# A second layer issued from one written list of steps, with chunk 1 transposed by DMA

## The chip, the cores and the metric

The kernel runs on one core of one Trainium2 chip. The metric is the device time of one launch in microseconds, median of three runs. Engine names are those of the profile: PE (TensorE matmul), PEld (its weight loads), DVE (VectorE), ACT (ScalarE), POOL (GpSimd), SP (SyncE, which issues every DMA of this part).

## The reference, cut to what matters

An attention-like recurrence gives 3072 rows of 384 numbers, a first gated layer (two products, their elementwise product, a third and fourth product) follows, and then the second layer, which is all that the change touches:

```python
h = x @ w_in                                  # 3072 x 384 by 384 x 1024
e = np.exp(h - np.max(h, axis=-1, keepdims=True))
solu = h * e / (np.sum(e, axis=-1, keepdims=True) + 1e-09)
ln = (solu - mean(solu)) / np.sqrt(var(solu) + 1e-06) * g_ln
out = ln @ w_out                              # 3072 x 1024 by 1024 x 384
```

## The kernel before, in words

The second layer works in 24 chunks of 128 rows. Every float32 product is made of three matmuls of split operands (high by high, high by low, low by high: lines 200 to 202, one helper). The order of each engine's instructions is the order in which the code is written; no scheduler moves them here. The work on one chunk i, with the letter that the change gives to each step, is this:

- **s**: x2 is split, high part on ACT (L842), low part on POOL (L843).
- **h**: 18 matmuls of 512 columns on PE into the accumulator `ps_h` (there are two, one for even and one for odd chunks).
- **e**: the row maximum `nm` on DVE (L855), then the exponential on ACT (L858).
- **m**: on DVE the product `p` of `ps_h` and `e` (L863; after it `ps_h` is free for chunk i+2), the statistics (L866 to L876), and two small operations on POOL.
- **c**: the mean is taken off, on ACT (L885).
- the chunk is transposed, in one of two ways. By PE, **t**: 8 transposes (L927) into `ps_p`. By DMA, **v**: ACT takes the chunk apart into 16-bit halves (L896, four copies), SP stores them in DRAM in two halves (L897, tile `pd`) and reads each half back transposed (L902, tile `e`).
- **u** (after t) or **w** (after v): the transposed chunk is split into `pt`, high part on ACT (L350, two casts), low part on DVE (L527, two subtractions).
- **o**: 24 matmuls of 384 columns on PE from `pt` into `ps_o`.
- **z**: the scaled result on ACT (L947) and its store by SP (L948).

Chunks 0 and 1 and the last one (23) were transposed by PE, chunks 2 to 22 by DMA. A loop over i issued h, e, s, m of chunk i+1, then w and o, z of an earlier chunk, then c and v of chunk i+1. Exceptions in it (`M0`, `M1`) moved w of chunks 2 and 21 and left out one o at i = 3. Before the loop, while the first layer ends, h, e, m and c of chunk 0 are issued. After the loop, and ahead of the last three results, every engine reads the flag `wok` into a register (L1214), on which a branch around a slow fallback path depends.

Of the kernel before, what the change touches and what calls it, by code (L numbers as in the profile page):

```python
# [8 lines left out]
F32 = mybir.dt.float32  # L9
# [115 lines left out]
def tile_rwkv_bilinear_solu(  # L125
# [710 lines left out]
    def pick(i):  # L836
        return pq[i % len(pq)]
# [5 lines left out]
        nc.gpsimd.tensor_sub(xl, x, f32(xh))  # L843
        return xh, xl

    def s3(x, i=0, between=None, ahead=NCH):
        xh, xl = x
        wih, wil = d2["wih"], d2["wil"]
        q = pick(i)["q"]
        ph = pick(i)["h"].tile([P, 2, NH], F32, name="ps_h", tag="ps_h")  # L850
        for hf in range(2):
            hsl = slice(hf * NH, (hf + 1) * NH)
            mm3(ph[:, hf, :], [((xh[:, kt, :], xl[:, kt, :]), (wih[:, kt, hsl], wil[:, kt, hsl])) for kt in range(KM)])
        nm = q.tile([P, 1], F32, name="nm", tag="nm")
        nc.vector.tensor_reduce(out=nm, in_=ph, axis=AX.XY, op=ALU.max, negate=True)  # L855
        e = pq[min(i % 3, 1)]["q"].tile([P, 2, NH], F32, name="e", tag=f"e{i % 3}")
        sm = q.tile([P, 1], F32, name="sm", tag="sm")
        nc.scalar.activation(e, ph, AF.Exp, bias=nm, scale=1.0, accum_out=sm)  # L858
        if between:
            between()  # L860
        split_chunk(ahead)
        p = q.tile([P, 2, NH], F32, name="p", tag="p")
        nc.vector.tensor_mul(p, ph, e)  # L863
        st = q.tile([P, 2, 6], F32, name="bst", tag="bst")
        for hf in range(2):
            nc.vector.bn_stats(st[:, hf, :], p[:, hf, :])  # L866
# [12 lines left out]
        a = q.tile([P, 1], F32, name="al", tag="al", bufs=2)
        nc.gpsimd.tensor_mul(a, rs, c1)  # L880
        return e, p, nmean, a, i

    def center(st):
        e, p, nmean, a, i = st
        nc.scalar.activation(e, p, AF.Identity, bias=nmean, scale=1.0)  # L885
        return e, a, i, p

    def move(pc):

        e, a, i, p = pc  # L890
        ev = e.bitcast(U16).rearrange("t a (f k) -> t a f k", k=2)
        pv = p.bitcast(U16).rearrange("t a (k f) -> t a k f", k=2)
        d = pld.tile([2, P, 2, NH], U16, name="pd", tag="pd", bufs=2)
        for hf in range(2):
            for k in range(2):
                nc.scalar.copy(pv[:, hf, k, :], ev[:, hf, :, k])  # L896
            nc.sync.dma_start(d[hf], pv[:, hf])  # L897
        x = e.rearrange("p a (k t) -> p (a k) t", t=P)
        xv = x.bitcast(U16)
        for hf in range(2):  # L900
            sl = slice(hf * (KF // 2), (hf + 1) * (KF // 2))
            nc.sync.dma_start_transpose(xv[:, sl, :], d[hf].rearrange("t k f -> (t k) f"))  # L902
        return x, a, i

    def pt_tile(i):
        if i % len(pq):
            return const.tile([P, 2, KF, P], F32R, name="pt", tag="ox")
        return pq[0]["q"].tile([P, 2, KF, P], F32R, name="pt", tag="pt")

    def moved(mv):  # L910
        x, a, i = mv
        t = pt_tile(i)
# [5 lines left out]
    def s4_T(pc):
        e, a, i, _ = pc
        pv = e.rearrange("t a f -> t (a f)")  # L920
        t = pt_tile(i)
        th, tl = t[:, 0], t[:, 1]
        for hf in range(2):
            ps = pick(hf)["p"].tile([P, KF // 2, P], F32, name="ps_p", tag="ps_p")
            for j in range(KF // 2):
                kf = hf * (KF // 2) + j
                nc.tensor.transpose(ps[:, j, :], pv[:, kf * P:(kf + 1) * P], ident)  # L927
            sl = slice(hf * (KF // 2), (hf + 1) * (KF // 2))
            run(split(ps, th[:, sl, :], tl[:, sl, :]))
        return th, tl, a, i  # L930

    def s4_mm(pT, ps, part, parts):
        th, tl = pT[:2]
        woh, wol = d2["woh"], d2["wol"]
        if part == 0:
            ps = pq[-1]["p"].tile([P, DM], F32, name="ps_o", tag="ps_o", bufs=len(pq))
        kfs = range(part * KF // parts, (part + 1) * KF // parts)
        mm3(
            ps, [((th[:, kf, :], tl[:, kf, :]), (woh[:, kf, :], wol[:, kf, :])) for kf in kfs],
            start=part == 0, stop=part == parts - 1,  # L940
        )
        return ps

    def s4_out(pT, ps, dst):
# [3 lines left out]
        nc.sync.dma_start(dst, o)  # L948

    def s4(pT, dst):  # L950
        s4_out(pT, s4_mm(pT, None, 0, 1), dst)

    def split_chunk(i):
        if i < NCH:
# [4 lines left out]
        row = b * S + c * P  # L959
        return out[row:row + P, :]  # L960

    xs, sm, pT = {}, {}, {}
    pld = ctx.enter_context(tc.tile_pool(name="pld", bufs=1, space=bass.MemoryType.DRAM))
    qsb, qps = ExitStack(), ExitStack()

# [177 lines left out]
    for c in range(NG, NC):  # L1143
        last = c == NC - 1
        for ft in range(KF):
            if c == 2 and ft == 3:
                with tc.tile_pool(name="wr", bufs=1, side="right") as wr:
                    w_ok(wr)

            if c == NC - 2 and ft == FT2:  # L1150
                uc = ubase = NU
                open_phase2()
                nlim = len(units)
                cv_load(uc)
# [24 lines left out]
            if last and ft == KF - 1:  # L1179
                st = s3(xs[0])  # L1180
            if pend is not None:
                s2(*pend)
            if late and turn_over:
                cvstep()
            pend = (c, ft)
            if last and ft == KF - 1:
                s2(*pend)
                sm[0] = center(st)
        if c == NC - 2:
            x2t[1] = const.tile([P, NCH - X2A, KM, P], F32, name="x2c", tag="xa")  # L1190
    f1.close()


    open_q(qsb, qps, "left", 1)
    def turn(i):
        pT[i] = s4_T(sm[i])

    M0, M1 = 2, NCH - 1
    split_chunk(2)
    for i in range(NCH - 1):  # L1200
        st = s3(xs[i + 1], i + 1, None if i else (lambda: turn(0)), i + 3)
        if M0 < i - 1 < M1 - 2:
            pT[i - 1] = moved(pT[i - 1])
        n = i - 1 if i <= M0 else i - 2
        if n >= 0 and i != M0 + 1:
            s4(pT[n], out_rows(n))
        if 0 < i < M0:
            turn(i)
        sm[i + 1] = center(st)
        if i in (M0, M1 - 2):  # L1210
            pT[i] = moved(pT[i])
        if M0 <= i + 1 < M1:
            pT[i + 1] = move(sm[i + 1])
    ok = nc.values_load(wok[0:1, 0:1], min_val=0, max_val=1)  # L1214
# [10 lines left out]
    with tc.If(ok < 1):  # L1225
# [52 lines left out]
        with tc.For_i(0, B * S, P) as row:  # L1278
# [96 lines left out]
```

## Time and profile before

| | us |
|---|---|
| median of 3 runs (lowest, highest) | 654.43 (654.26, 656.4) |
| the profiled execution's own time | 654.89 |
| its span, from first to last instruction | 653.1 |
| busy in the span: PE, DVE, ACT, POOL | 635.4, 411.7, 344.3, 267.0 |

The table says how long each engine had an instruction under way. Matmul records overlap (one of 512 columns is shown with some 0.39 us and the next starts 0.23 us later), so a start-to-start distance says more than a record's length. The second layer's first matmul starts at 431.31 us of the span.

### The profile page before, as it was taken

To read this page: it belongs to the slowest core of one execution; us is meant where nothing else is said; L and a number is where in the kernel's file an instruction comes from. 1 tells how busy PE (TensorE), PEld (TensorE's weight loads), DVE (VectorE), ACT (ScalarE), POOL (GpSimd) and SP (SyncE) were. 2 spreads that over 40 slices of the span, in tenths; PEclk is the share of its full clock that TensorE was granted. 3 is DMA by queue.
4 is the path that set the end of the run, shared out by engine and by line. 5 is a ranking of instruction groups with operands and counts; after the bars stand their busy time and mean duration, and the time that the engine had idled before them with its cause. 6 is when DMAs were issued, how large, how long until landed. Compare 5 with 4: busy or idle time off the path is not lost.

```text
span 653.1 us, 12130 instructions
## 1 busy us (share of the span) xinstructions
PE 635.4 (97%) x4652; PEld 541.4 (83%) x4652; DVE 411.7 (63%) x731; ACT 344.3 (53%) x684; POOL 267.0 (41%) x267
## 2 busy tenths in 40 slices
PE   8989999999999999999999999999979999999996
PEld 8867778998878888888888887788868888889996
DVE  8999998765764433333344277536676777777771
ACT  5576876552323222322232366435676778777772
POOL 3888664430333554555565355422122222222210
PEclk9999999999999999999999999999989999999999
DMA  8889687533543222222220333000555556566561
GB/s 288 246 285 306 224 262 240 174 125 120 160 151 98 69 69 70 69 70 70 69 85 16 126 127 120 2 1 12 110 150 145 145 146 149 143 153 148 159 153 41
DMA packets 94721, 86.45 MB, mean 132 GB/s; under 512 B 49857, under 2 KB 76226, under 8 KB 94658
## 3 DMA queue, kind: packets, MB, share of 16 engines
q1 hardware_dynamic: 94658, 85.62, 44.5%
q8 instruction: 38, 0.62, 0.4%
q14 instruction: 25, 0.20, 0.1%
HBM read 54.67 MB, written 19.92 MB: 114 GB/s over the span
## 4 chain that ended last, share of the span: by engine, by line
PE 75%; DVE 12%; ACT 4%; POOL 3%; issue 2%; DMA 2%; SPq 0%; DVEq 0%; POOLq 0%; ACTq 0%
PE ps_o L202 5%; PE ps_o L200 5%; PE ps_o L201 5%; PE ps_x L200 5%; PE ps_h L202 4%; PE ps_h L201 4%; PE ps_h L200 4%; PE ps_x L202 4%; PE ps_x L201 4%; PE ps_aa L200 4%; PE ps_aa L201 4%; PE ps_bb L200 4%; PE ps_aa L202 4%; PE ps_bb L201 4%; PE ps_bb L202 4%; PE ps_a L369 3%
## 5 line engine op out<-in xcount | busy, mean ns | idle before, releaser
L727 DVE TENSOR_TENSOR g<-ps_bb,a 128x512 f32<-128x512 f32 x48 | 32.9, 686 | 92.9 <-PE ps_bb L202 91.9
L512 POOL TENSOR_TENSOR cvm<-cvm,cvq 128x384 int32<-128x384 int32 (+1 forms) x54 | 66.7, 1241 | 43.2 <-DVE cvm L508 36.1
L350 ACT COPY a<-ps_aa 128x512 f32<-128x512 f32 x46 | 26.8, 583 | 80.4 <-PE ps_aa L202 80.4
L202 PE MATMUL ps_o<-woh,pt 128*128 128x384 f32 x192 | 65.7, 342 | 3.0 <-DVE pt L527 2.8
L200 PE MATMUL ps_o<-woh,pt 128*128 128x384 f32 x192 | 65.7, 342 | 1.5 <-ACT pt L350 1.5
L738 POOL TENSOR_TENSOR gl<-g,gh 128x512 fp32r<-128x512 f32 x32 | 41.2, 1287 | 62.8 <-ACT gh L733 62.8
L201 PE MATMUL ps_o<-wol,pt 128*128 128x384 f32 x192 | 65.4, 340 | 0.0
L200 PE MATMUL ps_bb<-x,w2h 128*128 128x512 f32 x144 | 57.2, 397 | 2.6 <-DVE g L727 2.6
L200 PE MATMUL ps_x<-gh,wc 128*128 128x512 f32 x144 | 58.3, 405 | 0.0
L200 PE MATMUL ps_aa<-x,w1h 128*128 128x512 f32 x144 | 57.1, 397 | 0.2
L202 PE MATMUL ps_h<-wih,x2l 128*128 128x512 f32 x144 | 57.2, 397 | 0.0
L201 PE MATMUL ps_h<-wil,x2h 128*128 128x512 f32 x144 | 56.8, 395 | 0.0
L200 PE MATMUL ps_h<-wih,x2h 128*128 128x512 f32 x144 | 56.8, 394 | 0.0
L201 PE MATMUL ps_aa<-x,w1h 128*128 128x512 f32 x144 | 56.2, 391 | 0.3 <-DVE x L527 0.3
L202 PE MATMUL ps_x<-gh,wc 128*128 128x512 f32 x144 | 56.3, 391 | 0.0
L201 PE MATMUL ps_bb<-x,w2h 128*128 128x512 f32 x144 | 56.1, 390 | 0.0
L201 PE MATMUL ps_x<-gl,wc 128*128 128x512 f32 x144 | 56.1, 390 | 0.0
L202 PE MATMUL ps_bb<-x,w2l 128*128 128x512 f32 x144 | 56.1, 390 | 0.0
L202 PE MATMUL ps_aa<-x,w1l 128*128 128x512 f32 x144 | 56.1, 390 | 0.0
L733 ACT CAST gh<-g 128x512 fp32r<-128x512 f32 x32 | 19.9, 621 | 60.0 <-DVE g L727 57.8
L878 POOL TENSOR_TENSOR rs<-vs,nhalf 128x1 f32<-128x1 f32 x24 | 20.1, 839 | 72.3 <-DVE vs L876 72.3
L863 DVE TENSOR_TENSOR p<-ps_h,e 128x1024 f32<-128x1024 f32 x24 | 29.4, 1224 | 31.2 <-ACT e L858 31.2
(172 smaller groups left out, 1584.1 us busy)
## 6 DMA issues: line engine op xcount, KB each, us to landing
pd<-p SPq DMA_DIRECT2D x42, 256.0 KB, 2.0
cvs<-in_w_T_dram SPq DMA_DIRECT2D x16, 512.0 KB, 4.4
cvs<-in_w_dram SPq DMA_DIRECT2D x16, 384.0 KB, 5.2
kT<-in_k_T_dram SPq DMA_DIRECT2D x20, 256.0 KB, 2.7
rT<-in_r_T_dram SPq DMA_DIRECT2D x20, 256.0 KB, 3.8
v_in<-in_v_dram SPq DMA_DIRECT2D x24, 192.0 KB, 4.0
k_in<-in_k_dram SPq DMA_DIRECT2D x24, 192.0 KB, 3.1
out_dram<-o SPq DMA_DIRECT2D x24, 192.0 KB, 2.0
```

What stands on the lines that cost most here:

```text
L200: nc.tensor.matmul(dst, lhsT=ah, rhs=bh, start=start and i == 0, stop=False)
L201: nc.tensor.matmul(dst, lhsT=ah, rhs=bl, start=False, stop=False)
L202: nc.tensor.matmul(dst, lhsT=al, rhs=bh, start=False, stop=stop and i == last)
L350: (e.copy if e is nc.scalar else e.tensor_copy)(dst, src)
L369: nc.tensor.matmul(pso[o][:, p, :], lhsT=kT[n][sl, p, :], rhs=rT[n][sl, p, :], start=True, stop=True)
L512: nc.gpsimd.tensor_tensor(mi, mi, q, op=ALU.add)
L727: nc.vector.tensor_mul(gt[c, ft], pb, at[c, ft])
L733: nc.scalar.copy(gt[c, ft][1], gt[c, ft][0])
L738: e.tensor_sub(gl, g, f32(gh))
L863: nc.vector.tensor_mul(p, ph, e)
L878: nc.gpsimd.tensor_tensor(rs, vs, pq[0]["nhalf"], op=ALU.pow)
```

## The change

`ORDER` is one string of 214 steps: a letter for the step, a number for the chunk. `issue` walks it and calls the function of each step, so that `s3` and `s4_T` are cut into the steps above (`s3_mm`, `s3_exp`, `s3_stats`, `turn`, `parts`). The part ahead of "|" is issued where the first layer ends, the rest in place of the loop. Chunk 1 now stands in the list as v and w (by DMA) in place of t and u, chunks 0 and 23 stay with PE, and `pd` has four buffers in place of two. The flag `wok` is read after the whole list.

```diff
+ORDER = (
+    'h0 e0 | h1 m0 c0 s2 t0 s3 h2 e1 m1 u0 c1 h3 v1 e2 o0 s4 s5 e3 m2 c2 v2 m3 h4 w1 c3 s6 h5 e4 z0 v3 o1 s7 m4 w2 '
+    'h6 c4 e5 v4 s8 z1 m5 w3 o2 h7 c5 e6 s9 v5 m6 o3 w4 h8 z2 c6 z3 o4 e7 m7 s10 w5 v6 c7 e8 v7 h9 z4 o5 m8 s11 h10 '
...
+    'h22 v21 o18 e22 h23 z18 m22 z17 w20 c22 o19 o20 v22 e23 w21 z19 o21 m23 z20 c23 t23 w22 u23 z21 o22 o23 z23 '
+    'z22 '
+)
...
-        d = pld.tile([2, P, 2, NH], U16, name="pd", tag="pd", bufs=2)
+        d = pld.tile([2, P, 2, NH], U16, name="pd", tag="pd", bufs=4)
...
+    def issue(order):
+
+        for x in order.split():
+            kind, i = x[0], int(x[1:])
+            if kind == "s":
+                split_chunk(i)
+            elif kind == "h":
+                now[i] = s3_mm(xs[i], i)
+            elif kind == "o":
+                acc[i] = s4_mm(now[i])
+            elif kind == "z":
+                s4_out(now[i], acc[i], out_rows(i))
+            else:
+                fn = {"e": s3_exp, "m": s3_stats}.get(kind)
+                now[i] = fn(now[i], i) if fn else {"c": center, "t": turn, "v": move, "u": parts, "w": parts}[kind](now[i])
...
             if last and ft == KF - 1:
-                st = s3(xs[0])
+                issue(ORDER.split("|")[0])
...
-    M0, M1 = 2, NCH - 1
-    split_chunk(2)
-    for i in range(NCH - 1):
-        st = s3(xs[i + 1], i + 1, None if i else (lambda: turn(0)), i + 3)
-        if M0 < i - 1 < M1 - 2:
-            pT[i - 1] = moved(pT[i - 1])
-        n = i - 1 if i <= M0 else i - 2
-        if n >= 0 and i != M0 + 1:
-            s4(pT[n], out_rows(n))
-        if 0 < i < M0:
-            turn(i)
-        sm[i + 1] = center(st)
-        if i in (M0, M1 - 2):
-            pT[i] = moved(pT[i])
-        if M0 <= i + 1 < M1:
-            pT[i + 1] = move(sm[i + 1])
+    issue(ORDER.split("|")[1])
     ok = nc.values_load(wok[0:1, 0:1], min_val=0, max_val=1)
-    pT[NCH - 2] = moved(pT[NCH - 2])
-    s4(pT[NCH - 3], out_rows(NCH - 3))
-    turn(NCH - 1)
-    for i in (NCH - 2, NCH - 1):
-        s4(pT[i], out_rows(i))
```

Three places show what the list moves. The first is DVE at the start of the second layer. Before, from the maximum of chunk 1 (`nm_4842`) to the maximum of chunk 2 (`nm_4905`); `pt_4847` is the split of chunk 0:

```order
L855 TENSOR_REDUCE nm_4842<-ps_h_4823 128x1
L527 TENSOR_TENSOR pt_4847<-ps_p_4848,pt_4847 128x512
L527 TENSOR_TENSOR pt_4847<-ps_p_4855,pt_4847 128x512
L863 TENSOR_TENSOR p_4866<-ps_h_4823,e_4844 128x1024
L866 BN_STATS bst_4868<-p_4866 128x6 x2
...
L876 TENSOR_SCALAR vs_4878<-vs_4878 128x1
L855 TENSOR_REDUCE nm_4905<-ps_h_4886 128x1
```

After, the same stretch, up to the product `p_4976` of chunk 2 (`nm_4875`, `p_4880` are chunk 1, `pt_4899` is chunk 0, `nm_4933` and `nm_4971` are chunks 2 and 3):

```order
L869 TENSOR_REDUCE nm_4875<-ps_h_4799 128x1
L879 TENSOR_TENSOR p_4880<-ps_h_4799,e_4877 128x1024
...
L892 TENSOR_SCALAR vs_4892<-vs_4892 128x1
L538 TENSOR_TENSOR pt_4899<-ps_p_4842,pt_4899 128x512
L538 TENSOR_TENSOR pt_4899<-ps_p_4847,pt_4899 128x512
L869 TENSOR_REDUCE nm_4933<-ps_h_4856 128x1
L869 TENSOR_REDUCE nm_4971<-ps_h_4905 128x1
L879 TENSOR_TENSOR p_4976<-ps_h_4856,e_4935 128x1024
```

Chunk 0's two subtractions moved behind chunk 1's product and statistics, and chunk 3's maximum moved ahead of chunk 2's product.

The second place is ACT around the split of chunk 3. Before, from the casts of chunk 2 (`pt_5062`) to those of chunk 3 (`pt_5180`, which reads `e_5007`); `e_5097` is chunk 4, `e_5154` is chunk 5:

```order
L350 CAST pt_5062<-e_4907 128x512 x2
L896 COPY p_5014<-e_5007 128x512 x4
L858 ACTIVATE e_5097,sm_5098<-ps_h_5076,nm_5095 128x1024
L842 CAST x2h_5100<-x2b_2189 128x384
L885 ACTIVATE e_5097<-p_5104,nmean_5111 128x1024
L896 COPY p_5104<-e_5097 128x512 x4
L858 ACTIVATE e_5154,sm_5155<-ps_h_5133,nm_5152 128x1024
L842 CAST x2h_5157<-x2b_2189 128x384
L350 CAST pt_5180<-e_5007 128x512 x2
```

After, from the split of chunk 1 (`pt_5043`) over that of chunk 2 (`pt_5137`) to that of chunk 3 (`pt_5202`, which reads `e_4973`); `e_5074` is chunk 4, `e_5164` chunk 5:

```order
L361 CAST pt_5043<-e_4877 128x512 x2
...
L872 ACTIVATE e_5074,sm_5075<-ps_h_5024,nm_5072 128x1024
L958 ACTIVATE o_5077<-ps_o_4938,al_4835 128x384
L915 COPY p_5005<-e_4973 128x512 x4
L853 CAST x2h_5114<-x2b_2189 128x384
L361 CAST pt_5137<-e_4935 128x512 x2
L904 ACTIVATE e_5074<-p_5118,nmean_5125 128x1024
L872 ACTIVATE e_5164,sm_5165<-ps_h_5053,nm_5162 128x1024
L915 COPY p_5118<-e_5074 128x512 x4
...
L361 CAST pt_5202<-e_4973 128x512 x2
```

Chunk 3's copies for the DMA moved from behind chunk 2's split to ahead of it, and behind chunk 4's exponential.

The third place is ACT at the end. Before, from chunk 23's centring (`e_6775`) on:

```order
L885 ACTIVATE e_6775<-p_6778,nmean_6785 128x1024
L1214 TENSOR_LOAD wok_61
L350 CAST pt_6840<-e_6684 128x512 x2
L947 ACTIVATE o_6870<-ps_o_6845,al_6618 128x384
L350 CAST pt_6873<-ps_p_6874 128x512
L350 CAST pt_6873<-ps_p_6881 128x512
L947 ACTIVATE o_6913<-ps_o_6888,al_6704 128x384
L947 ACTIVATE o_6941<-ps_o_6916,al_6795 128x384
```

After, the same stretch (the last three results are those of chunks 21, 23 and 22):

```order
L904 ACTIVATE e_6791<-p_6827,nmean_6834 128x1024
L361 CAST pt_6860<-e_6677 128x512 x2
L361 CAST pt_6865<-ps_p_6850 128x512
L361 CAST pt_6865<-ps_p_6855 128x512
L958 ACTIVATE o_6870<-ps_o_6802,al_6605 128x384
L958 ACTIVATE o_6923<-ps_o_6898,al_6844 128x384
L958 ACTIVATE o_6926<-ps_o_6873,al_6719 128x384
L1222 TENSOR_LOAD wok_61
```

The result of chunk 22 moved behind that of chunk 23, and the flag's load moved behind everything.

## Rows read from the trace of the kernel before

**Rows 1.** The page: busy time and share of the span of each engine.
```profile
PE 635.4 (97%) x4652; PEld 541.4 (83%) x4652; DVE 411.7 (63%) x731; ACT 344.3 (53%) x684; POOL 267.0 (41%) x267
```

**Rows 2.** PE's longest wait from 430 us on: total, times, longest.
```profile
PE ps_o L202 <- DVE pt L527: 2.8, 1, 2.8
```

**Rows 3.** Windows: PE, PEld, DVE, ACT, POOL busy; granted clock, DMA share, GB/s.
```profile
480.00:485.00 5.00, 0.94 (x3) 0.62 (x4) 4.52 (x11) 3.79 (x8) 1.92 (x2) 0.85 0.76 196
485.00:490.00 5.00, 5.00 (x17) 5.00 (x17) 3.48 (x5) 4.25 (x9) 1.23 (x3) 0.50 0.48 145
...
500.00:520.00 20.00, 20.00 (x99) 17.72 (x99) 14.81 (x34) 15.53 (x26) 5.42 (x8) 1.00 0.55 145
```

**Rows 4.** The chain that ended last, 463 to 485 us: start, length, what.
```profile
463.33 5.51 DMA e<-pd
468.86 0.62 ACT pt L350
469.48 2.08 ACT p L896 x4
...
479.14 1.11 ACT e L858 x2
...
483.93 0.70 DVE pt L527
```

**Rows 5.** Timeline of PE: start, length; the first matmul of a block.
```profile
448.91 0.34 PE L200 MATMUL ps_o<-woh,pt 128*128 128x384 f32 x1
...
453.08 1.03 PE L927 MATMUL ps_p<-ident,e 128*128 128x128 f32 x8
453.87 0.48 PE L200 MATMUL ps_h<-wih,x2h 128*128 128x512 f32 x1
...
458.16 0.34 PE L200 MATMUL ps_o<-woh,pt 128*128 128x384 f32 x1
...
462.75 0.40 PE L200 MATMUL ps_h<-wih,x2h 128*128 128x512 f32 x1
...
466.95 0.39 PE L200 MATMUL ps_h<-wih,x2h 128*128 128x512 f32 x1
...
471.15 0.34 PE L200 MATMUL ps_o<-woh,pt 128*128 128x384 f32 x1
...
475.34 0.40 PE L200 MATMUL ps_h<-wih,x2h 128*128 128x512 f32 x1
...
491.19 0.40 PE L200 MATMUL ps_h<-wih,x2h 128*128 128x512 f32 x1
```

**Rows 6.** Timelines of ACT and DVE at the start of the second layer.
```profile
445.37 1.11 ACT L858 ACTIVATE e<-ps_h,nm 128x1024 f32<-128x1024 f32 x1 [2.54 <-DVE nm L855]
...
457.49 1.15 ACT L885 ACTIVATE e<-p,nmean 128x1024 f32<-128x1024 f32 x1 [1.26 <-DVE c L872]
458.67 2.18 ACT L896 COPY p<-e 128x512 uint16<-128x512 uint16 x4
...
454.42 1.22 DVE L863 TENSOR_TENSOR p<-ps_h,e 128x1024 f32<-128x1024 f32 x1 [1.27 <-ACT e L858]
...
458.07 1.28 DVE L527 TENSOR_TENSOR pt<-ps_p,pt 128x512 fp32r<-128x512 f32 x2
459.26 1.21 DVE L855 TENSOR_REDUCE nm<-ps_h 128x1 f32<-128x1024 f32 x1
```

**Rows 7.** Transposing DMAs, issue to landing: chunk 2 (461 to 469), then 490 to 640.
```profile
DMA to landing us min/median/max: 6.0/6.0/6.0
...
DMA to landing us min/median/max: 3.2/3.6/5.7
```

**Rows 8.** The end: timeline of ACT; SP's load of the flag; SP's last wait.
```profile
647.50 0.58 ACT L947 ACTIVATE o<-ps_o,al 128x384 f32<-128x384 f32 x1 [3.58 <-PE ps_o L202]
...
L1214 SPq TENSOR_LOAD <-wok x1: 482/482/482, 635.5 to 635.5; - x1
...
SPq L1225 <- SPq L1225: 2.7, 1, 2.7
```

More of the change, by code (lines that the diff above doesn't have):

```diff
@@ L844, in x2_split, with s3_mm @@
         return xh, xl
-    def s3(x, i=0, between=None, ahead=NCH):
+    def s3_mm(x, i=0):
         xh, xl = x
         wih, wil = d2["wih"], d2["wil"]
-        q = pick(i)["q"]
         ph = pick(i)["h"].tile([P, 2, NH], F32, name="ps_h", tag="ps_h")
@@ L853, in s3, with s3_exp @@
             mm3(ph[:, hf, :], [((xh[:, kt, :], xl[:, kt, :]), (wih[:, kt, hsl], wil[:, kt, hsl])) for kt in range(KM)])
+        return ph
+    def s3_exp(ph, i=0):
+        q = pick(i)["q"]
         nm = q.tile([P, 1], F32, name="nm", tag="nm")
@@ L858, in s3, with s3_stats @@
         nc.scalar.activation(e, ph, AF.Exp, bias=nm, scale=1.0, accum_out=sm)
-        if between:
-            between()
-        split_chunk(ahead)
+        return ph, e, sm
+    def s3_stats(x, i=0):
+        ph, e, sm = x
+        q = pick(i)["q"]
         p = q.tile([P, 2, NH], F32, name="p", tag="p")
@@ L881, in s3 @@
         return e, p, nmean, a, i
+    def s3(x):
+        return s3_stats(s3_exp(s3_mm(x)))
     def center(st):
@@ L902, in move, with turn @@
             nc.sync.dma_start_transpose(xv[:, sl, :], d[hf].rearrange("t k f -> (t k) f"))
-        return x, a, i
-    def pt_tile(i):
-        if i % len(pq):
[L907 to L912, printed above, removed]
+        return [x[:, 0:KF // 2], x[:, KF // 2:]], a, i
+    def turn(pc):
+        e, a, i, _ = pc
+        pv = e.rearrange("t a f -> t (a f)")
+        ps = []
+        for hf in range(2):
+            t = pick(hf)["p"].tile([P, KF // 2, P], F32, name="ps_p", tag="ps_p")
+            for j in range(KF // 2):
+                kf = hf * (KF // 2) + j
+                nc.tensor.transpose(t[:, j, :], pv[:, kf * P:(kf + 1) * P], ident)
+            ps.append(t)
+        return ps, a, i
@@ L913, in moved, with parts @@
+    def parts(mv):
+        src, a, i = mv
+        if i % len(pq):
+            t = const.tile([P, 2, KF, P], F32R, name="pt", tag="ox")
+        else:
+            t = pq[0]["q"].tile([P, 2, KF, P], F32R, name="pt", tag="pt")
         for hf in range(2):
             sl = slice(hf * (KF // 2), (hf + 1) * (KF // 2))
-            run(split(x[:, sl, :], t[:, 0, sl, :], t[:, 1, sl, :]))
+            run(split(src[hf], t[:, 0, sl, :], t[:, 1, sl, :]))
         return t[:, 0], t[:, 1], a, i
[L918 to L930, printed above, removed]
@@ L932, in s4_mm @@
-    def s4_mm(pT, ps, part, parts):
+    def s4_mm(pT):
         th, tl = pT[:2]
         woh, wol = d2["woh"], d2["wol"]
[L935 to L941, printed above, removed]
+        ps = pq[-1]["p"].tile([P, DM], F32, name="ps_o", tag="ps_o", bufs=len(pq))
+        mm3(ps, [((th[:, kf, :], tl[:, kf, :]), (woh[:, kf, :], wol[:, kf, :])) for kf in range(KF)])
@@ L950, in s4 @@
     def s4(pT, dst):
-        s4_out(pT, s4_mm(pT, None, 0, 1), dst)
+        s4_out(pT, s4_mm(pT), dst)
     def split_chunk(i):
@@ L960, in out_rows @@
         return out[row:row + P, :]
-    xs, sm, pT = {}, {}, {}
+    xs, now, acc = {}, {}, {}
+    def issue(order):
[9 more added lines that the diff above has]
+                s4_out(now[i], acc[i], out_rows(i))
+            else:
+                fn = {"e": s3_exp, "m": s3_stats}.get(kind)
+                now[i] = fn(now[i], i) if fn else {"c": center, "t": turn, "v": move, "u": parts, "w": parts}[kind](now[i])
     pld = ctx.enter_context(tc.tile_pool(name="pld", bufs=1, space=bass.MemoryType.DRAM))
@@ L1187, in tile_rwkv_bilinear_solu @@
                 s2(*pend)
-                sm[0] = center(st)
         if c == NC - 2:
@@ L1194, in tile_rwkv_bilinear_solu @@
     open_q(qsb, qps, "left", 1)
-    def turn(i):
-        pT[i] = s4_T(sm[i])
-    M0, M1 = 2, NCH - 1
-    split_chunk(2)
-    for i in range(NCH - 1):
-        st = s3(xs[i + 1], i + 1, None if i else (lambda: turn(0)), i + 3)
-        if M0 < i - 1 < M1 - 2:
-            pT[i - 1] = moved(pT[i - 1])
-        n = i - 1 if i <= M0 else i - 2
-        if n >= 0 and i != M0 + 1:
-            s4(pT[n], out_rows(n))
-        if 0 < i < M0:
-            turn(i)
-        sm[i + 1] = center(st)
-        if i in (M0, M1 - 2):
-            pT[i] = moved(pT[i])
-        if M0 <= i + 1 < M1:
-            pT[i + 1] = move(sm[i + 1])
-    ok = nc.values_load(wok[0:1, 0:1], min_val=0, max_val=1)
-    pT[NCH - 2] = moved(pT[NCH - 2])
-    s4(pT[NCH - 3], out_rows(NCH - 3))
-    turn(NCH - 1)
-    for i in (NCH - 2, NCH - 1):
-        s4(pT[i], out_rows(i))
+    issue(ORDER.split("|")[1])
+    ok = nc.values_load(wok[0:1, 0:1], min_val=0, max_val=1)
     qps.close()
@@ L1308, in tile_rwkv_bilinear_solu @@
             nc.scalar.copy(xf, px)
-            s4(s4_T(center(s3(x2_split(xf)))), out[bass.ds(row, P), :])
+            s4(parts(turn(center(s3(x2_split(xf))))), out[bass.ds(row, P), :])
         fx.close()
```

4 rows, old and new, of the table ORDER are left out of this document.

## Prediction

> **What bounds the kernel now.** I read the page first, then PE's waits, then the windows, then the chain, then the timelines. PE is busy for 97% of the span [rows 1], so a change of order can only win back what PE loses. In the second layer PE runs without a break from 485 us to its last block, and its one serious wait is for a split `pt` on DVE, 2.8 us in one piece [rows 2]. The windows place it: between 480 and 485 us PE is busy for 0.94 of 5.00 us, and in the next five the granted clock is 0.50, the lower of TensorE's two levels (1.2 in place of 2.4 GHz), after that idleness [rows 3].
>
> The price is read from the starts of PE's blocks [rows 5]. From 466.95 to 475.34 us lie one h and one o (chunks 5 and 2): 4.20 + 4.19 = 8.39 us. From 475.34 to 491.19 us lie the same two kinds (h of chunk 6, o of chunk 3): 15.85 us. So wait and slow clock together cost 15.85 − 8.39 = **7.46 us**.
>
> The chain tells why [rows 4]. Chunk 2's transposed data landed late: 5.51 us from the second half's issue. ACT takes instructions in order, and chunk 2's casts stood ahead of chunk 3's four copies (469.48) and, by the loop, of everything of chunks 4 and 5. The exponential of chunk 5 started at 479.14, and chunk 3's casts stood behind it, its subtractions behind chunk 5's product and statistics (483.93). PE had come to o of chunk 3 at 475.34 + 4.20 = 479.54.
>
> **The change, part by part.** *Chunk 1 leaves PE.* Eight transposes go: next block at 453.87 after 453.08, 0.79 us, and 0.09 for the matmul behind them, which took 0.32 us in place of 0.23 to its successor (0.48 long in place of 0.39 [rows 5]): **0.88 us**. Its own o took 4.59 us (458.16 to 462.75) in place of 4.19, a short wait for its split: **0.40 us** more if the new place of the split has it ready.
>
> *The new start, placed step by step.* Durations [rows 6]: exponential 1.11; product 1.22; from a product's start to its centring on ACT 457.49 − 454.42 = 3.07, to DVE's next work 458.07 − 454.42 = 3.65; two subtractions 1.19; maximum 1.21; centring to copies 1.18; copies 2.18.
> - Chunk 1's exponential ends at 446.5, as before. Its product no longer stands behind chunk 0's subtractions: 446.6 to 447.8. `ps_h` is then free for h3, which PE can take when h2 ends, 448.9: spare 1.1 us.
> - Chunk 0's subtractions now come at 446.6 + 3.65 = 450.25, done 451.4; o0 starts at 448.9 + 4.2 = 453.1: spare 1.7.
> - Chunk 3's maximum is now ahead of chunk 2's product on DVE. It waits for h3's end, 453.1, and ends at 454.4; the product of chunk 2 runs 454.5 to 455.7. h4 needs that at 457.3: spare 1.6. Chunk 3's product is done at 454.5 + 3.65 + 1.22 = 459.4, h5 needs it at 461.5: spare 2.1.
> - Chunk 1 by DMA: centring 446.6 + 3.07 = 449.7, copies 450.9. For chunk 2, the first trip before, copies to the last subtraction took 458.67 to 469.48 + 0.70, 11.5 us, with 6.0 us from issue to landing [rows 4, 6, 7]. That puts chunk 1's split at 462.4. On ACT its casts stand behind chunk 2's copies (454.5 + 3.07 + 1.18 + 2.18 = 460.9), which gives 462.8. o1 starts at 453.1 + 4.19 + 4.20 + 4.20 = 465.7: spare 2.9.
> - o3, where the stall was: PE comes to it at 465.7 + 2 × 8.39 = 482.5. Before, chunk 3's casts had to wait behind chunk 2's DMA; now its copies stand ahead of them. Its subtractions come directly behind chunk 5's statistics: chunk 4's product at 465.2, chunk 2's subtractions to 470.0, maximum of 5 to 471.3, exponential to 472.4, product and statistics to 476.1, subtractions to 477.3. Spare 5.2. So I set the stall at nothing, and nothing comes in its place at these steps.
>
> *The steady part.* ACT works 15.53 and DVE 14.81 of 20 us while PE is full [rows 3]; per chunk of 8.39 us that is 6.5 and 6.2 us, so both keep some 1.9 us spare and no change of their order alone can make them the bound. The number of instructions is the same, but for two more pairs of a DMA round trip (one store and one transposing load for each half of chunk 1), four copies on ACT at the start (2.18 us, inside the placement above) and PE's eight transposes. DMA engines are used at 0.55 [rows 3]. What does change is cover: before, five blocks of PE lay between a chunk's copies and its o; in the list it is three to five, and two for chunks 12 and 22 (8.4 us), with copies sometimes issued for two chunks close together. Copies to split takes 11.5 us with a landing of 6.0 and 11.5 − 2.4 = 9.1 with the median of 3.6 [rows 7]. ACT must then run ahead of PE by about a microsecond at these two, which its spare time lets it do. I take nothing, and keep 0 to 4.0 us as the bounds: from no wait up to one wait of some 2 us, with the low clock after it. In the window at 0.50 stand 17 matmuls [rows 3], 5.00 / 17 = 0.29 us each in place of 4.19 / 24 = 0.175: that clock cost 17 × 0.12 = 2.0 us there.
>
> *SP's queue and `pd`.* Copies, transposes and results stand on SP in the list's order; a transpose waits there for its store, and results queue behind it. A result's store has nobody waiting but the next result but one of its parity, 16.8 us later. Two more buffers of `pd` take away a wait that the trace does not show on PE's path: nothing.
>
> *The end.* The result of chunk 22 now follows chunk 23's on ACT, where it was done during the last o: at most one more pass, 0.58 us **later** [rows 8]. The flag's load on SP (0.48 us) moves behind the last store; SP waits there 2.7 us for landings anyhow [rows 8], so nothing; were that cover gone it would be 0.48 us.
>
> *Sum.* 7.46 + 0.88 + 0.40 − 0.58 = 8.16 us. The profiled execution of 654.89 us becomes 646.7; it lay 0.46 above the median of 654.43, so the median becomes **646.2 us**. About 0.3% (2 us) is what a measurement of this kernel can tell from no change.
>
> **A rule against it.** PE's waits fall on a chunk that went by DMA, and never on a chunk that PE turned for more than 0.4 us [rows 2, 5]; the trip costs 9.1 to 11.5 us. The Trainium skill, "VectorE: DVE Perf Modes", section "Rules for kernel authors", says to transpose a 128×128 block on TensorE where a PSUM destination will do, and to use the DMA otherwise. By that rule chunk 1 should have stayed; the trace agrees that the way by DMA is longer, and what it would do here is rival 1.
>
> **The rivals.**
> 1. *Chunk 1 comes late.* It becomes the first trip, and the first is the slow one (6.0 against 3.6 us [rows 7]). For it: that difference. Against: 2.9 us of spare. It decides above a landing of 8.9 us. At twice the landing, 12 us, PE waits 3.1 us and then runs at the low clock: 646.2 + 3.1 + 2.0 = 651.3 us; with a short wait 647 to 649. Chance 5%.
> 2. *One wait in the list's later part* (chunks 12, 22, or two chunks' copies close together). For it: less cover, landings up to 5.7 us [rows 7]. Against: 1.9 us spare per chunk. With 2 us of wait and the clock 646.2 + 4.0 = 650.2 us. Chance 13%.
> 3. *The stall only moves* to another o at full size: 7.46 are back, 646.2 + 7.46 = 653.7, within 0.3%. For it: DVE and ACT are the releasers, and they have as much work as before. Against: the placement. Chance 4%.
> 4. *Slower: transposes land late throughout*, since stores and loads of two chunks now meet on the queues. The place is ACT's casts, where a late landing blocks all of ACT. Up to 3.6 + 1.9 = 5.5 us a landing is swallowed by ACT's spare time; above, each of 22 chunks pays. At 6.0, as the first did, 22 × 0.5 = 11 us: 657.2 us. It ends above the time before from some 5.9 us on. For it: 5.7 did occur. Against: the median of 3.6 and DMA engines at 0.55. Chance 6%.
>
> **How the numbers follow.** The forecast, PE without a wait from the list's first step to its last, has 72%; its own range is 645.4 to 647.8 us: 0.8 down if the last pass costs nothing and a run falls a little low, 1.6 up for short waits at a few of the 1-us spares. The range for 8 in 10 reaches down to 645.2 and up to 650.8, which takes in rival 2 and the shorter half of rival 1. Faster by over 0.3%: 72 + 5 + 13 = 90%; within 0.3%: 4%; slower: 6%.
>
> **What would show it.** PE's waits after 431 us should hold no entry above half a microsecond and no window below full clock; o1 should start near 465.7, o3 near 482.5, and the pass on ACT that follows PE's last matmul, at 647.50 us before [rows 8], should start some 8.7 us earlier. Two results should run on ACT directly one behind the other at the end. ACT waiting for `e<-pd` and PE for `pt` would show rival 1 or 2 by their chunk; landings near 6 us throughout, rival 4. The prediction is wrong if PE's blocks are not 8.39 us per pair from 448.9 us on.

## The result and the profile after

The changed kernel takes 647.53 us (median of 6 runs, 646.91 to 650.31) against 654.47 us before (6 runs, 653.09 to 656.4): ratio 0.9902, 95% interval [0.9877, 0.9926]. The forecast was 646.2 us with a range of 645.2 to 650.8. The profiled execution took 647.47 us, its span is 645.6 us.

Runs of one kernel differ by 1 to 7 us, and a part of that arises ahead of the second layer: its first matmul starts at 430.3 to 433.1 us in the profiled executions of this study. So I read three things of each profile: the start of that matmul, the start of the last product's result pass on ACT, and the end of the span. The span from the first to the last of them is called the **segment** below. Before, they lie at 431.31, 647.50 and 653.1 us; after, at 431.30, 638.65 and 645.6. The segment fell from 221.8 to 214.3 us: 216.19 − 207.35 = 8.84 us were won up to the last pass, and 6.95 − 5.60 = 1.35 us lost behind it.

The page of the changed kernel, busy time by engine, and the granted clock in 40 slices:

```profile
PE 632.1 (98%) x4644; PEld 539.8 (84%) x4644; DVE 408.7 (63%) x731; ACT 342.7 (53%) x688; POOL 268.4 (42%) x267
...
PEclk9989999999999999999999999999999999999998
```

DVE has the same number of instructions as before [rows 1], ACT four more (chunk 1's copies) and PE eight fewer (its transposes). PE's view of waits holds no entry at all from 429 us to the end. The windows where the stall was [rows 3]:

```profile
480.00:485.00 5.00, 5.00 (x27) 4.50 (x26) 3.53 (x9) 3.12 (x8) 1.56 (x2) 1.00 0.23 69
485.00:490.00 5.00, 5.00 (x26) 4.36 (x25) 3.05 (x4) 4.30 (x8) 0.24 (x1) 1.00 0.71 200
500.00:520.00 20.00, 20.00 (x104) 18.36 (x103) 15.09 (x33) 15.86 (x27) 5.95 (x9) 1.00 0.74 174
```

PE is busy for all of the first two windows, at full clock. The timeline of PE, the first matmuls of h4 and of o1, o2 and o3:

```profile
457.27 0.40 PE L211 MATMUL ps_h<-wih,x2h 128*128 128x512 f32 x1
...
465.67 0.34 PE L211 MATMUL ps_o<-woh,pt 128*128 128x384 f32 x1
...
474.06 0.34 PE L211 MATMUL ps_o<-woh,pt 128*128 128x384 f32 x1
...
482.44 0.34 PE L211 MATMUL ps_o<-woh,pt 128*128 128x384 f32 x1
```

The blocks stand 8.39 and 8.38 us apart, from the new start on. The timeline of ACT at the start: chunk 1's exponential, centring, copies and casts, then the exponential of chunk 4, the copies of chunk 3 and the casts of chunk 2:

```profile
445.36 1.12 ACT L872 ACTIVATE e<-ps_h,nm 128x1024 f32<-128x1024 f32 x1 [1.00 <-DVE nm L869]
...
449.67 1.15 ACT L904 ACTIVATE e<-p,nmean 128x1024 f32<-128x1024 f32 x1 [2.14 <-DVE c L888]
450.85 2.18 ACT L915 COPY p<-e 128x512 uint16<-128x512 uint16 x4
...
460.78 1.14 ACT L361 CAST pt<-e 128x512 fp32r<-128x512 f32 x2
...
464.30 1.12 ACT L872 ACTIVATE e<-ps_h,nm 128x1024 f32<-128x1024 f32 x1 [0.93 <-DVE nm L869]
...
465.87 2.17 ACT L915 COPY p<-e 128x512 uint16<-128x512 uint16 x4
...
468.36 1.14 ACT L361 CAST pt<-e 128x512 fp32r<-128x512 f32 x2
```

Neither of the two casts ends an idle time: the transposed data is there when ACT comes to it. Its landing, for the transposing DMAs of the first stretch (453 to 462 us):

```profile
DMA to landing us min/median/max: 3.4/3.4/3.7
```

So the first trip is no longer the slow one (6.0 before [rows 7]). The end: the timeline of ACT, SP's own load of the flag with the register operation behind it, its branch and the first of the events that end the program, and SP's last wait:

```profile
638.65 1.05 ACT L958 ACTIVATE o<-ps_o,al 128x384 f32<-128x384 f32 x2 [7.32 <-PE ps_o L213]
...
L1222 SPq TENSOR_LOAD <-wok x1: 525/525/525, 640.1 to 640.1; - x1
L1222 SPq FUSED_REGOPS  x1: 181/181/181, 640.7 to 640.7; - x1
...
L1228 SPq EVENT_SEMAPHORE  x8: 17/17/17, 643.7 to 644.2; - x8
...
L1228 SPq COMPARE_BRANCH  x1: 53/53/53, 641.0 to 641.0; - x1
...
SPq L1228 <- SPq L1228: 2.6, 1, 2.6
```

The same two instructions of the kernel before:

```profile
L1225 SPq EVENT_SEMAPHORE  x8: 17/17/17, 651.2 to 651.7; - x8
...
L1225 SPq COMPARE_BRANCH  x1: 53/53/53, 648.5 to 648.5; - x1
```

From the start of the last product's pass to SP's branch it was 648.5 − 647.50 = 1.0 us, and is 641.0 − 638.65 = 2.35. From the branch to the events it is 2.7 us in both. The wait that was to cover the load starts behind the load.

### The profile page after: what moved, and what is told of

It reads as the page before. It is cut to its first block, busy times and chain, and to the rows that moved or that the text cites. A ratio compares the mean times of both kernels' runs of the same rounds, so it can differ in the third digit from the quotient of the medians.

```text
span 645.6 us, 12190 instructions
## 1 busy us (share of the span) xinstructions
PE 632.1 (98%) x4644; PEld 539.8 (84%) x4644; DVE 408.7 (63%) x731; ACT 342.7 (53%) x688; POOL 268.4 (42%) x267
## 4 chain that ended last, share of the span: by engine, by line
PE 90%; DVE 3%; DMA 2%; POOL 1%; ACT 1%; issue 1%; SPq 0%; POOLq 0%; ACTq 0%; DVEq 0%
PE ps_x L211 5%; PE ps_h L213 5%; PE ps_h L212 5%; PE ps_o L211 5%; PE ps_o L212 5%; PE ps_o L213 5%; PE ps_h L211 5%; PE ps_x L213 5%; PE ps_x L212 5%; PE ps_bb L211 5%; PE ps_aa L211 5%; PE ps_bb L213 5%; PE ps_bb L212 5%; PE ps_aa L212 4%; PE ps_aa L213 4%; PE ps_a L380 3%
## 5 line engine op out<-in xcount | busy, mean ns | idle before, releaser
L211 PE MATMUL ps_o<-woh,pt 128*128 128x384 f32 x192 | 64.5, 336 | 0.0
L213 PE MATMUL ps_o<-woh,pt 128*128 128x384 f32 x192 | 64.3, 335 | 0.0
```

The lines of the kernel that those rows point to most:

```text
L211: nc.tensor.matmul(dst, lhsT=ah, rhs=bh, start=start and i == 0, stop=False)
L213: nc.tensor.matmul(dst, lhsT=al, rhs=bh, start=False, stop=stop and i == last)
```

## The experiments

The theory after the result: the start, the way of chunk 1 and the order around o3 give what the sum says, and the flag's load is what the sum left out. Rivals: chunk 1 by DMA gives nothing or costs; the whole list is needed; the stall had another cause than the prediction named. On that cause theory 1 is the prediction's: chunk 3's copies stood behind chunk 2's DMA. Theory 2: it is the order of the later work on ACT, which gave chunk 3's casts their turn only behind chunk 5's exponential. Theory 3, formed after e5: PE's own order. The table holds all runs; "to last pass" is the time from the second layer's first matmul to the last product's result pass on ACT, "behind it" from there to the span's end.

| kernel | ratio to before, 95% interval | to last pass | behind it | segment |
|---|---|---|---|---|
| before | | 216.19 | 5.60 | 221.8 |
| changed | 0.9902 [0.9877, 0.9926] | 207.35 | 6.95 | 214.3 |
| e0_after, the changed kernel again | 0.9904 [0.9885, 0.9923] | 207.35 | 6.78 | 214.1 |
| e1_end_order | 0.9909 [0.9891, 0.9928] | 207.35 | 6.36 | 213.7 |
| e7_flag_early | 0.9911 [0.9884, 0.9938] | 207.35 | 6.07 | 213.4 |
| e8_flag_and_end_order | 0.9885 [0.9859, 0.9912] | 207.35 | 5.71 | 213.1 |
| e2_chunk1_by_PE | 0.9919 [0.9900, 0.9938] | 208.21 | 6.81 | 215.0 |
| e4_new_start_only | 0.9915 [0.9892, 0.9939] | 208.44 | 6.57 | 215.0 |
| e5_old_start_new_from_o1 | 0.9927 [0.9902, 0.9952] | 208.62 | 6.78 | 215.4 |
| e3_old_order_as_list | 1.0029 [1.0005, 1.0053] | 214.07 | 6.32 | 220.4 |
| e6_old_order_swap | 1.0028 [1.0008, 1.0048] | 216.41 | 6.46 | 222.9 |
| e11_old_order_h_ahead | 0.9983 [0.9956, 1.0010] | 214.08 | 6.39 | 220.5 |
| e9_stores_doubled | 0.9912 [0.9882, 0.9942] | 207.35 | 6.79 | 214.1 |
| e10_two_pd_buffers | 0.9911 [0.9880, 0.9943] | 207.35 | 6.78 | 214.1 |

Where PE has no wait, the time to the last pass repeats to 0.01 us: seven profiled executions at 207.35. That is why the segment tells apart what the medians cannot. Each kernel that stalls has one profile alone, and these differ in how late chunk 2's transposes landed (4.8 to 6.0 us), so their segments are rougher.

### The way of chunk 1

**e0_after** is the changed kernel unchanged. 

> The changed kernel once more, beside the others on one chip. Theory (all that PE lost in the second layer is won back, and the end takes some 1.3 us longer than before): 647.0 to 648.0 us median, 6.4 to 7.5 us below the kernel before; PE without a wait from 431 us on. Rival (the gain hangs on when the transposing DMAs happen to land): runs spread by several us, and PE waits for the split pt in the profile.

It takes 647.82 us, to the last pass 207.35 again, and PE does not wait.

**e2_chunk1_by_PE**: chunk 1 goes back to PE, in the new list.

```diff
-... m1 u0 c1 h3 v1 e2 ...  h4 w1 c3 ...
+... m1 u0 c1 h3 e2 ...  h4 t1 u1 c3 ...
```

> The changed list, but chunk 1 turned by PE (t1 u1 where w1 stood, v1 gone). Theory (the trip by DMA is hidden, the eight transposes are not): 0.8 to 1.0 us above the changed kernel, no wait of PE. Rival (the page's rule, TensorE where it can): equal or faster, since four copies on ACT and four DMAs go.

It takes 649.26 us, 207.35 becomes 208.21, and PE waits in neither kernel. Chunk 1's way by DMA is worth 0.86 us here, which is what its transposes take on PE; nothing of the DMA trip shows.

### Which part of the list

**e3_old_order_as_list** is the old loop written as a list (chunk 1 by PE, `pd` with four buffers, the flag's load behind the list). 

> The loop's order of before written as a list and issued by the changed code, chunk 1 by PE; flag read at the end, pd with four buffers. Theory (order alone made the gain): as the kernel before, with the wait of PE for the split of chunk 3 of some 4 to 5 us and the low clock after it; from the first matmul of the second layer to the span's end 221.8 to 222.8 us, the upper value if the flag's late load costs 0.8 us. Rival (four buffers of pd or the list's form gave part of it): 219 us or less.

It takes 654.73 us and stalls at the same place, 2.8 us for a split and 0.4 for its cast at o3 (1.5 before), with a granted clock of 0.66 in the window behind. The written list alone gives nothing. Its segment, 220.4 us, is below the 221.8 to 222.8 of the theory and above the rival's 219: chunk 2's transposes landed in 4.8 us in this execution and in 6.0 in the profiled one of before [rows 7], which goes with the shorter wait.

**e4_new_start_only** keeps the new list up to h10 and then goes on in the pattern of the old loop. 

> The changed list up to h10, then the loop's regular pattern of before for the rest, with its end (z22 ahead of o23). Theory (the only place where PE lost time is before chunk 8, so the rest of the list is worth nothing by itself): PE waits at most some 1.3 us more where the two patterns meet, and the end is shorter by 0.5 to 1.3 us: between 1.3 us below and 1 us above the changed kernel. Rival (the whole list is needed, the loop's pattern loses time at a steady rate): 3 us or more above it.

It takes 648.73 us, with one wait of 0.7 us (for a split, at 513.90 us). The list's later order is worth 208.44 − 207.35 = 1.1 us, no more.

**e5_old_start_new_from_o1** is its counterpart: the old order up to o1, the new list from there on.

```diff
-h0 e0 | h1 m0 c0 s2 t0 s3 h2 e1 ... v3 o1 s7 m4 w2 h6 c4 e5 ...
+h0 e0 | m0 c0 s2 h1 e1 t0 u0 s3 m1 c1 h2 e2 s4 m2 o0 z0 t1 u1 c2 v2 h3 e3 s5 m3 o1 h4 c3 s6 h5 e4 v3 s7 m4 w2 h6 c4 e5 ...
```

> The old order up to o of chunk 1 (chunk 1 by PE), the new list from there on. Theory 2 (the old stall at o of chunk 3 came from the order of the steps of chunks 2 to 5 between o1 and o3, where the casts of chunk 3 stood on ACT behind the exponential of chunk 5): although chunk 2 is again the first chunk by DMA and its copies are as late as before, PE has no wait over 0.5 us at o3, and from the second layer's first matmul to the span's end it is some 216 us (214.3 of the changed kernel, and 0.9 for PE's eight transposes, 0.4 for the short wait at o1, and short waits of the old start). Rival (the stall comes from the late start of chunk 2's trip, so from the old beginning): 2 to 3 us of wait on PE at o2 or o3 with the low clock behind it, 219 to 222 us.

It takes 649.00 us. There is no wait at o3, though chunk 2 is again first by DMA and lands in 4.9 us. To the last pass it takes 208.62, which is 1.27 more than the changed kernel: 0.88 for PE's eight transposes and 0.40 for the short wait at o1 make 1.28. The rest of the gain up to the last pass, 216.19 − 208.62 = 7.57 us, is the stall, and it lies in the order of the steps behind o1.

### Which order made the stall

**e6_old_order_swap** tries the prediction's words on it: in e3, chunk 3's copies for the DMA move ahead of chunk 2's casts.

```diff
-... o1 z1 c3 w2 v3 h4 ...
+... o1 z1 c3 v3 w2 h4 ...
```

> The same old order with one swap: chunk 3's copies and DMA ahead of chunk 2's split on ACT (v3 w2 in place of w2 v3). Theory 1, as the prediction put it (chunk 3 was late since its copies stood behind chunk 2's DMA): the wait for chunk 3 goes, 5 us or more below the old order as a list. Theory 2 (its casts wait for their turn on ACT behind chunk 5's exponential, which is late since ACT's work of chunks 4 and 5 hangs on chunk 2's split as before, so a swap of neighbours does not help): within 1 us of it, same wait.

It takes 655.57 us. PE's waits and the windows:

```profile
PE ps_o L213 <- DVE pt L538: 2.8, 1, 2.8
PE ps_o L211 <- ACT pt L361: 1.5, 1, 1.5
...
480.00:485.00 5.00, 0.85 (x3) 0.30 (x2) 4.01 (x10) 3.82 (x7) 1.41 (x2) 0.96 0.74 180
485.00:490.00 5.00, 4.81 (x15) 4.82 (x16) 3.48 (x5) 4.73 (x10) 1.74 (x3) 0.50 0.41 146
```

The stall stands in full (chunk 2's transposes landed in 5.6 us here). So it was not the place of chunk 3's copies alone.

**e11_old_order_h_ahead** changes only PE's order in e3: from chunk 2 on, h of chunk n + 4 stands ahead of o of chunk n, as in the new list at this place.

```diff
-... s7 m5 w3 o2 z2 c5 v5 h6 e6 s8 m6 w4 o3 z3 c6 v6 h7 e7 ...
+... s7 m5 w3 h6 o2 z2 c5 v5 e6 s8 m6 w4 h7 o3 z3 c6 v6 e7 ...
```

> The list of the old order, in which only PE's order is changed: from chunk 2 on, h of chunk n + 4 stands ahead of o of chunk n in place of behind it, as it does in the new list at this place (h6 o2 h7 o3 in place of o2 h6 o3 h7); every other engine keeps the old order. Theory 3 (the stall at o3 came from PE's own order: it reached o3 with one h too few ahead of it, while the chain over ACT from chunk 2's DMA to chunk 3's split was as long as ever): PE has no wait for a split at o3. By the rows of the old order it has one wait of 1.7 us instead, at h6, for chunk 4's product (done at 474.1, PE ready at 472.4), and then none, since chunk 5's product is done at 481.6 and h7 is due at 482.5. PE is then 3.7 us ahead of the old order, 220.4 - 3.7 = 216.7 us from the second layer's first matmul to the span's end, up to 218 if the clock falls at the wait. Rival (theory 2, the order on ACT and DVE is what counts): the wait only changes its name, to h6 and h7 waiting for products, and the segment stays at 219.5 to 222.

It takes 653.03 us, no different from before, with the flag's late load in it, and its segment is that of e3. PE's waits, with columns as in [rows 2], and ACT's timeline from chunk 2's casts to chunk 4's exponential:

```profile
PE ps_h L210 <- DVE p L878: 2.8, 1, 2.8
PE ps_p L932 <- ACT e L903: 1.2, 1, 1.2
PE ps_o L212 <- DVE pt L537: 0.7, 1, 0.7
...
470.25 0.62 ACT L360 CAST pt<-e 128x512 fp32r<-128x512 f32 x1 [0.28 <-DMA e<-pd]
470.78 2.17 ACT L914 COPY p<-e 128x512 uint16<-128x512 uint16 x4
472.86 1.10 ACT L871 ACTIVATE e<-ps_h,nm 128x1024 f32<-128x1024 f32 x1
```

The wait at o3 is gone, as theory 3 says. In its place PE waits at h6 for chunk 4's product, 2.8 us where I expected 1.7: chunk 2's transposes landed in 6.0 us here, as in the kernel before, and in 4.8 in e3, whose rows I had taken. The 0.7 and 1.2 us come only at 627.69 and 637.13, at the list's end. So the total hides what the order did at the stall. PE's first matmul behind the same work (h of chunks 0 to 11, o of chunks 0 to 7), from the timelines of the kernel before, e3, e11 and e5:

```profile
528.94 0.34 PE L200 MATMUL ps_o<-woh,pt 128*128 128x384 f32 x1
...
528.13 0.34 PE L211 MATMUL ps_o<-woh,pt 128*128 128x384 f32 x1
...
525.83 0.40 PE L210 MATMUL ps_h<-wih,x2h 128*128 128x512 f32 x1
...
521.65 0.40 PE L211 MATMUL ps_h<-wih,x2h 128*128 128x512 f32 x1
```

Counted from the second layer's first matmul (431.31, 432.61, 432.73 and 431.50) these are 97.63, 95.52, 93.10 and 90.15 us. Measured against e5, the stall costs 7.48 us before, 5.37 in e3 and 2.95 in e11. PE's order alone thus wins 2.4 us against e3, and 4.5 against the kernel before, which had the same landing as e11. From this point to the last pass e3 takes 118.55 us and e11 120.98, so the two waits at the end give 2.4 us back. The rival was right on the segment and not on the reason; theory 3 holds for some half of the stall or more, and falls as the sole cause. What is left shows in the rows: chunk 4's exponential stands on ACT behind chunk 2's casts, as in all old orders, and these wait for the DMA. In e5, whose landing is late too, the same three steps stand in another order:

```profile
468.61 1.12 ACT L872 ACTIVATE e<-ps_h,nm 128x1024 f32<-128x1024 f32 x1 [0.93 <-DVE nm L869]
...
469.72 2.17 ACT L915 COPY p<-e 128x512 uint16<-128x512 uint16 x4
...
472.20 1.15 ACT L361 CAST pt<-e 128x512 fp32r<-128x512 f32 x2
```

Counted from the first matmul, chunk 4's exponential starts at 37.11 us in place of 40.13 in e11; the casts come behind it and find their data landed. Chunk 3's casts start no earlier in e5 than in e3, at 48.60 and 48.14 us. But PE comes to o3 at 52.42 us, and in e3 at 48.21 (44.01, the start of h6, and 4.20), because in e5 h7 stands ahead of it. For h7 the accumulator must be free, which needs chunk 5's exponential: at 44.53 us, and 46.63 in e3. So theory 2 holds in a wider form, and the new list works by two things at once: exponentials ahead of casts that wait for a DMA, and one h more ahead of each o. The copies' place alone (e6) gives nothing. PE's order alone (e11) gives 4.5 of 7.5 us at the stall by the kernel before, 2.4 of 5.4 by e3. That the rest belongs to ACT's order is read from the rows of e11 and e5, and a part of it goes with the landing (6.0 us in e11, 4.9 in e5); ACT's new order with PE's old one was not run.

### The end

**e1_end_order**: the result of chunk 22 before chunk 23's, as before.

```diff
-... o22 o23 z23 z22
+... o22 z22 o23 z23
```

> Chunk 22's result moved ahead of chunk 23's product in the list (o22 z22 o23 z23). Theory (the end of the changed kernel is longer because two passes and two stores of 192 KB follow one another after PE's last matmul): 0.5 us from the second pass, and up to 0.8 more from the last store landing alone; 0.5 to 1.3 us below the changed kernel. Rival (the end is longer because the flag's load now stands behind everything): at most 0.2 us.

**e7_flag_early**: the flag is read ahead of the last steps.

```diff
-    issue(ORDER.split("|")[1])
+    issue(ORDER.split("|")[1].split("w22")[0])
     ok = nc.values_load(wok[0:1, 0:1], min_val=0, max_val=1)
+    issue("w22" + ORDER.split("|")[1].split("w22")[1])
```

> The changed list, but the flag is read ahead of w22, as before. Theory (SP's late load and the two register operations behind it stand on the path to the end, since SP's last wait begins only at the branch behind them): 0.6 to 0.9 us less from the second layer's first matmul to the span's end, 213.4 us in place of 214.2. Rival, as the prediction had it (SP waits for landings anyhow): 214.2, no change.

**e8_flag_and_end_order** does both. 

> The flag early and the result of chunk 22 ahead of chunk 23's product, the rest of the list as changed. Theory: both terms add, 0.4 and 0.8 us: 213.0 us from the second layer's first matmul to the span's end, and 5.6 us from ACT's last pass to the end, as in the kernel before. Rival (they hide one another): 213.4 to 213.7 us.

The medians of e1 (648.51 us) and e7 (647.59) don't settle it, the segments do: 213.7 and 213.4 against 214.1 to 214.3 in four kernels with the end of the changed one. With both, 213.1. So e7 came out as its theory says, and e1 at the low end of the 0.5 to 1.3 us that I had set. SP's rows in e8:

```profile
L1222 SPq TENSOR_LOAD <-wok x1: 530/530/530, 626.0 to 626.0; - x1
...
L1229 SPq EVENT_SEMAPHORE  x8: 17/17/17, 642.3 to 642.8; - x8
L1229 SPq COMPARE_BRANCH  x1: 53/53/53, 639.5 to 639.5; - x1
```

Its one last pass starts at 638.49, so the branch follows 1.0 us later, as before the change, and the events 2.8 us behind it. From pass to branch the four kernels give 2.35 (changed), 1.9 (e1), 1.5 (e7) and 1.0 (e8): 0.45 to 0.5 for the second pass, 0.85 to 0.9 for the flag (0.53 for its load and the rest up to the branch). e8 takes 646.36 us (645.47 to 646.88), ratio 0.9885 [0.9859, 0.9912], and is the fastest of this study: it beats both kernels by its segment, though its interval overlaps that of the changed one.

### The cover of the DMA trips

**e9_stores_doubled** stores each half a second time, to a tile nobody reads. 

> The changed kernel; each half of each chunk is stored to DRAM a second time, into a tile that nobody reads, ahead of the store that counts (44 more stores of 256 KB on SP). If the cover of the DMA trips is as worked out (landings of the transposes up to some 5.5 us swallowed, more than that paid by every chunk), there are three cases by the landing that the trace shows: up to 4.5 us, no wait on PE over 0.5 us and the time within 1 us of the changed kernel; 4.5 to 5.5, a few short waits, 1 to 4 us; above 5.5 us throughout, rival 4's case, 22 times the excess, from 5 us up. I take the middle of the first two: 648 to 650. If the cover is much thinner than worked out, PE waits at every o and the time is above 655 with landings below 5 us.

The issues by DMA, size and median landing (455 to 640 us), and a window:

```profile
px<-p SPq DMA_DIRECT2D x42, 256.0 KB, 2.4
pd<-p SPq DMA_DIRECT2D x42, 256.0 KB, 2.8
...
e<-pd SPq DMA_TRANSPOSE x44, 3.6
...
500.00:520.00 20.00, 20.00 (x103) 18.22 (x102) 15.23 (x34) 15.59 (x27) 6.63 (x9) 1.00 0.83 244
```

42 of the 44 extra stores fall into this stretch and take the DMA share from 0.74 to 0.83. The store that counts lands in 2.8 us in place of 2.0, the transposes in 3.6 as ever, and PE does not wait: 648.09 us. I had named 648 to 650. That the loads themselves get slower, rival 4's case, could not be brought about in this way.

**e10_two_pd_buffers** gives `pd` two buffers again. 

> The changed kernel with two DRAM buffers of the transposed chunks in place of four. Forecast was that the further buffers are worth nothing: same within 0.3%, no wait on PE, the segment from the second layer's first matmul within 0.3 us of 214.3. Rival: the list issues copies of two chunks close together, so a store waits for the transposes two chunks back, SP stands still behind it, landings counted from issue grow and PE waits: 1 to 5 us slower.

It takes 648.04 us, segment 214.1, no wait: the further buffers are worth nothing here.

## Why the prediction was right, and where it was off

**The stall, 7.46 us: right.** Nothing came in its place; e5 isolates it at 7.57. The reading of [rows 2] left out a second wait of the same stall, the next entry of that view:

```profile
PE ps_o L200 <- ACT pt L350: 1.5, 1, 1.5
```

The price was read from the starts of blocks and holds both waits, so it stands: 4.3 us of waiting and, as an estimate, the remaining 3.1 for the slow clock behind them (7.46 less 4.36 by the timeline).

**Chunk 1, 0.88 and 0.40: right**, 0.86 by e2, and both together 1.27 by e5. Up to the last pass the sum says 7.46 + 0.88 + 0.40 = 8.74 us; 8.84 were measured.

**The placement: right.** o1 was set at 465.7 and o3 at 482.5, and started at 465.67 and 482.44; chunk 1's centring, copies and casts were set at 449.7, 450.9 and 460.9, and started at 449.67, 450.85 and 460.78.

**The end: mis-sized.** I had 0.58 us later; it is 1.35. The step that failed reads "SP waits there 2.7 us for landings anyhow [rows 8], so nothing". That wait begins at SP's branch in every kernel of the study (2.5 to 2.8 us from branch to events), so a load and its register operations ahead of the branch push its end back by all but 0.1 to 0.2 us. The price I had named for a lost cover, 0.48, was too small as well, since it counted the load without what follows it: 0.85 to 0.9 from pass to branch, 0.7 to 0.9 in the segment by e7. The second pass cost 0.4 to 0.6 by e1, as set. With 1.35 in place of 0.58 the sum is 7.39 us, 647.5 for the profiled execution, which took 647.47; that it fits to 0.03 is chance, since 0.10 us were missing up to the last pass. It lay below its median by 0.06 this time and the one of before 0.42 above its own, and so the forecast of the median was 1.3 us low.

**The cause of the old stall: half right.** The prediction said that the casts of chunk 2 stood on ACT ahead of chunk 3's copies "and, by the loop, of everything of chunks 4 and 5". The step on o3 named only the first, "chunk 3's casts had to wait behind chunk 2's DMA; now its copies stand ahead of them", and e6 takes that away without effect. The second half is what is left in e11, 2.95 us at h6. The other part, 4.5 of 7.5 us by the kernel before and 2.4 of 5.4 by e3, is PE's own order (e11), and this the prediction left unsaid: the list puts h7 ahead of o3. Its time for o3, 482.5, has h7 in it. So the stall was rightly set at nothing because the steps were placed one by one, and not because its cause was named.

**"The first is the slow one": wrong**, without effect on the sum. With chunk 1 first, at 454 us, the first trips landed in 3.3 to 3.9 us in the changed kernel, e0, e1 and e7; with chunk 2 first, from 462 us on, in 4.0 to 6.0 in the six kernels that do so. What makes those late is open.

**The rivals.** Rival 1: chunk 1's casts found their data at 460.78, and undoing the DMA cost 0.86 us. The rule of the Trainium skill ("VectorE: DVE Perf Modes", section "Rules for kernel authors"), a 128×128 transpose on TensorE where a PSUM destination will do, would have left chunk 1 with PE; e2 does that and is the slower one by these 0.86 us, so the measurement decides against it here, where PE is the bound and the trip is hidden. Rivals 2 and 3: no wait on PE at all. For chunk 22 the cover was even thinner than the prediction says: not two blocks, 8.4 us, but o21 and chunk 23's eight transposes, 4.16 + 0.79 = 4.95 us. Rival 4: landings of 3.5 us at the median, and no loss with the stores doubled.

## What to carry to other kernels

When one engine is full, write down when it needs each operand and what stands ahead of that operand's producer on its in-order queue; a cast that waits for a DMA belongs behind the work that feeds the full engine next, and the full engine's own order is the other half: e6 shows that moving the copies alone leaves the loss where it was, e11 that the full engine's order alone takes some half of it away. A total can hide such a gain when the same edit costs as much elsewhere, so compare two orders at a point where the same work is done. Work moved behind the last store of a program is on the path unless the wait that is to hide it starts earlier; read where that wait begins, not only how long it is. Where the start of a stage varies from run to run, compare from its first instruction on: 0.4 us could be told in this way, where medians differ by more from one set of runs to the next.

## What the hardware showed that I had not expected

SP's last 2.5 to 2.8 us, from the branch to the final events, are the same whether the last store was issued 0.1 us ahead of the branch (e8) or 0.9 us (changed), and with the DMA engines almost idle for the last of them (share 0.06 from 642 to 643 us after the change, the events at 643.7). The last store's landing is counted at 643.4 there (3.6 us from its issue at 639.7), and in every kernel of the study it lies at most 0.6 us ahead of the events, so a wait for it is not ruled out. Which event it waits for, the trace does not show.

Waits of 2.8 us had different prices. The windows of e11 and of e3, where the wait falls and behind it:

```profile
470.00:475.00 5.00, 2.71 (x12) 1.86 (x10) 3.43 (x4) 4.21 (x8) 0.47 (x1) 1.00 0.30 113
475.00:480.00 5.00, 4.54 (x20) 3.75 (x21) 3.75 (x10) 2.81 (x5) 1.26 (x3) 1.00 0.53 105
...
480.00:485.00 5.00, 1.73 (x8) 0.88 (x7) 4.32 (x11) 3.78 (x8) 1.72 (x2) 1.00 0.84 195
485.00:490.00 5.00, 5.00 (x20) 5.00 (x21) 3.48 (x5) 4.46 (x9) 1.43 (x3) 0.66 0.42 135
```

In e11 one wait of 2.8 us at h6, with PE busy for 2.71 of the 5 us from 470 us, was followed by a clock of 1.00. In e3 waits of 0.4 and 2.8 us, with two matmuls between them (1.73 of 5 us busy), were followed by 0.66, and in the kernel before 1.5 and 2.8 us (0.94 of 5 us busy) by 0.50. That is why a wait is better priced with the window that follows it than by its length.
